# Down projection of an attention + SwiGLU kernel: sums on VectorE in a fixed order, another product order, the first tile's value multiplied out of PSUM

## The chip, the cores and the metric

The kernel runs on one core of a Trainium2 chip (trn2). The metric is the device time of one execution in microseconds (us). The profile is of one execution; its engines are PE (TensorE matmul), PEld (TensorE weight load), DVE (VectorE), ACT (ScalarE), POOL (GpSimd) and SP (SyncE, which only issues transfers here).

## What is computed

An attention with rotary embedding over q, k, v of shape (4, 8, 576, 64), whose output is read as a matrix x of 2304 tokens by 512, and a gated projection on it:

```python
q_rot, k_rot = (rotate(q), rotate(k))
scores = scale * np.matmul(q_rot, k_rot.transpose(0, 1, 3, 2))
...
attn = np.exp(scores)
attn = attn / (np.sum(attn, axis=-1, keepdims=True) + 1e-09)
return np.matmul(attn, v).astype(np.float32)
...
g = x @ w_gate
silu = g * (1.0 / (1.0 + np.exp(-g)))
val = x @ w_val
return (silu * val @ w_out).astype(np.float32)
```

`w_gate` and `w_val` are 512 x 1536, `w_out` is 1536 x 512. All of it is fp32.

## The kernel before

Every fp32 factor is split into a high part (a cast by ACT) and a low part (source minus high part, a subtraction, most of them on DVE), and every product is three matmuls: high by high, high by low, low by high. Matmuls are 128x128 by 128x384: a block of tokens has BK = 384 columns.

Three stretches of the program matter here.

**Plain stage** (about 282 to 341 us). The attention is over and x stands in SBUF. For the first of NFP = 6 pairs of features, twelve units of plain matmuls (`mm`, L789) compute gate and value of one 128x384 block each. `ev` (L793 to L807) empties a unit's two PSUM banks: ACT applies Silu to the gate (L804), ACT copies the value (L805), and one transfer of 384 KB takes both to `hv` in DRAM. The value is multiplied on later. DVE at the same time makes splits and sums for the next stage. All engines run in program order there.

**Up stage** (about 337 to 563.7 us). The other five feature pairs go through a Strassen-Winograd scheme with seven products per 2x2 block (`unit`, L809; `finish`, L865). Tokens come in three pairs of blocks, taken in the order 1, 2, 0. PE and SP run in the order written; ACT, DVE and POOL are ordered by the tile scheduler. `Down.lead` gives a list of items (token pair, product, function) that are hooked into the last unit: the first loads and splits of the next stage. This is called the passage below.

**Down stage** (`Down.run`, L1399 to L1459). Three tiles of tokens, again seven products each, so 21 steps. A product has two halves j (128 output features each) of 6 x 3 matmuls, 36 in all, at L1437; 756 in the stage. Names that come up:

- `load` (L1358, L1360) and `late` (L1363): the four blocks B11, B12, B21, B22 of a tile, each 128 x 6 x 384, come from DRAM (`hv` for the gate of the first feature pair, `hd` for the others, `sg` from SBUF where the last pair of the first tile is still there). `vload` (L1351) brings the value of the first feature pair, `mult` (L1367) multiplies it on: on DVE for the first tile, on POOL for the others.
- `form` (L1377, L1378): for the step after the current one, the sum of blocks if that product needs one (L1373, one instruction of 128x2304, on DVE in the first tile and for one product of each tile, otherwise on POOL), then the split of the source in two halves of 128x1152: cast on ACT (L1377), subtraction on DVE (L1378). The results stand in two sets of buffers, so the split of a step can begin when the product before the running one is done.
- `osplit` (L1344 on ACT, L1345): the split of the seven `w_out` operands, 128x1536, in the first tile; the subtraction for all but the first two is on POOL.
- after a product: PSUM is copied by ACT (L1442, L1444, L1447) or added to an SBUF tile by DVE (L1440); POOL adds one more pair for `o22`. Results go out over SP (L1397).

ACT, DVE and POOL are ordered by the scheduler here too: it places each instruction by a model of times. In the lists of buffers, `dB`, `dT` are raw blocks and sums, `dH`, `dW`, `dWF` the split ones, `dO` split `w_out` operands, `du`, `dz`, `do` the tiles after a product.

Of the kernel before, what the change touches and what calls it, by code (L numbers as in the profile page):

```python
# [925 lines left out]
def attn_swiglu(ctx: ExitStack, tc: tile.TileContext, qk, vr, wg, wv, wo, main, tail, out):  # L926
# [4 lines left out]
    hd = [dr.tile([NFP - 1, 128, 4, BK], FP32, name=f"hd{p}") for p in range(3)]  # L931
    hv = [dr.tile([128, 4, 2, BK], FP32, name=f"hv{p}") for p in range(3)]
# [4 lines left out]
    moe = Moe(tc, keep, pl, yd, rd, hd, hv, od, wg, wv, wo, out)  # L937
# [168 lines left out]
    strassen(moe, J, S, Z).run()  # L1106
# [195 lines left out]
MULT = {4: ("B11",), 6: ("B21", "B12")}  # L1302
RAW = {"B11": ("T1h", 0), "B21": ("T1l", 2), "B12": ("T2h", 1), "B22": ("T2l", 3)}


class Down:
    def __init__(self, moe):
        self.moe, self.nc = moe, moe.nc
        self.raw, self.O, self.H, self.t, self.V = {}, {}, {}, {}, {}

    def lead(self):
        ve = self.nc.vector
        return [
            (0, 0, self.first), (0, 1, lambda: self.oload(0, slice(0, 5))), (0, 5, lambda: self.osplit(0, ve, slice(0, 5))),
            (1, 0, lambda: self.vload(0, "xb1")), (1, 0, lambda: self.load(0, "B11")),
            (1, 0, lambda: self.load(0, "B21")), (1, 4, lambda: self.late("B11")), (1, 4, lambda: self.late("B21")),
            (1, 4, lambda: self.oload(0, slice(5, 6))), (1, 4, lambda: self.oload(1)),
            (2, 0, lambda: self.load(0, "B12")), (2, 0, lambda: self.load(0, "B22")), (2, 0, lambda: self.late("B12")),
            (2, 0, lambda: self.late("B22")), (2, 0, lambda: self.mult(0, "B11", ve)),
            (2, 1, lambda: self.osplit(0, ve, slice(5, 6))),  # L1320
            (2, 1, lambda: self.form(0, ve)), (2, 4, lambda: self.mult(0, "B21", ve)), (2, 5, lambda: self.osplit(1, ve)),
        ]

    def first(self):
# [3 lines left out]
        self.O[0] = [x[:, 2304:3840].rearrange("p (f d) -> p f d", f=NFP) for x in (w, f)]  # L1328

    def oload(self, k, z=slice(0, NFP)):  # L1330
        a = self.moe.again
        if k == 4:
            self.O[4] = [self.w1[:, 2304:3840].rearrange("p (f d) -> p f d", f=NFP), a("FO", [128, NFP, 256], F32R, "dO")]
        elif k == 5:
            self.O[5] = [self.moe.r_p.tile([128, NFP, 256], F32R, name="R"), a("xm1", [128, NFP, 256], F32R, "dO")]
        elif k:
            s = {1: ("xa1h", "xa1l"), 2: ("xa2h", "xa2l"), 3: ("T0l0", "T0l1"), 6: ("xm2", "xm0")}[k]
            self.O[k] = [a(x, [128, NFP, 256], F32R, "dO") for x in s]
# [3 lines left out]
    def osplit(self, k, e, z=slice(0, NFP)):  # L1342
        Oh, Ol = (x[:, z] for x in self.O[k])
        self.nc.scalar.copy(Oh, r32(Ol))  # L1344
        e.tensor_tensor(out=Ol, in0=r32(Ol), in1=r32(Oh), op=ALU.subtract)  # L1345

    def vload(self, n, slot=None):
        m, p = self.moe, ORDER[n]
        for x in range(2):
            v = m.raw_p.tile([128, 2, BK], FP32, name="raw") if slot is None else                 m.again(f"{slot}{'hl'[x]}", [128, 2, BK], FP32, "dV")  # L1350
            self.nc.sync.dma_start(out=v, in_=m.hv[p][:, 2 * x:2 * x + 2, 1])  # L1351
            self.V[x] = v
# [16 lines left out]
    def form(self, s, e, se=None):
        k = s % 7  # L1370
        if k in SUMS:
            o, a, b = SUMS[k]
            se.tensor_tensor(out=self.raw[o], in0=self.raw[a], in1=self.raw[b], op=ALU.subtract)  # L1373
        src = self.raw[FORM[k]]
        hi, lo = self.H[s % 2]
        for z in (slice(0, 3), slice(3, NFP)):
            self.nc.scalar.copy(hi[:, z], src[:, z])  # L1377
            e.tensor_tensor(out=lo[:, z], in0=src[:, z], in1=r32(hi)[:, z], op=ALU.subtract)  # L1378

    def post(self, name, slot):  # L1380
        t = self.t[name] = self.moe.again(slot, [128, 2, BK], FP32, "d" + name)
        return t

    def open(self):
# [102 lines left out]
```

## Time and profile before

| | |
|---|---|
| runs | 724.43, 726.43, 725.01 us; median 725.01 |
| the profiled execution | 725.75 us, of which the profile's span is 724.0 us |
| PE busy over the span | 687.5 us (95%) |
| DVE, ACT, POOL busy | 593.7, 426.0, 541.0 us |
| first matmul of the Down stage | 563.69 us |
| first matmul of its second and third tile | 621.50, 671.99 us |
| start of the last matmul | 720.15 us |

The span is what the profiler saw of the execution; the execution's own time is 1.75 us longer, and it lies 0.74 us above the median. Times inside the program are counted from the start of the span. In a list of instructions the bracket at the end tells how long the engine was idle before it and what ended that; in a list of groups the idle time stands behind the second bar. PEclk is TensorE's granted clock, 1.00 for 2.4 GHz and 0.5 for 1.2 GHz; a value between is a stretch with both.

### The profile page before, as it was taken

The page shows a single profiled execution, that of the slowest core. Times are in us where ns is not written, and L with a number is a line of the kernel's source. Part 1 is how long each engine was busy: PE and PEld are TensorE (multiplying, and loading weights), DVE is VectorE, ACT ScalarE, POOL GpSimd, SP SyncE. Part 2 cuts the span into 40 slices and gives each one's busy share as a digit, 9 for nine tenths or more (in the row PEclk, how much of TensorE's full clock was granted, in tenths as well). Part 3 has the DMA queues.
Part 4 walks back from the last instruction along what each step waited for, and adds up shares of the span by engine and source line. Part 5 has one row for each costly group of instructions (what it writes and reads, how often), then busy time and mean ns, then how long its engine had stood idle before and what let it go on. Part 6 is the DMA issues. An engine that isn't in the chain of part 4 may idle for free. (4 is left out here: it accounts for less than half of the span.)

```text
span 724.0 us, 12703 instructions
## 1 busy us (share of the span) xinstructions
PE 687.5 (95%) x4414; PEld 668.3 (92%) x4414; DVE 593.7 (82%) x848; ACT 426.0 (59%) x873; POOL 541.0 (75%) x498
## 2 busy tenths in 40 slices
PE   7999999999999999997999999999999869899898
PEld 6999999999999998987999999999999768899897
DVE  5889898898888886849888979889886999498593
ACT  5899998888888885456444434444343454343341
POOL 8899799999999865749978695886846458544731
PEclk9999999999999999999999999999999989999999
DMA  6797899779888895962225354463557950733501
GB/s 197 209 223 204 219 226 254 202 212 251 225 204 202 201 265 159 212 215 88 80 95 190 103 178 178 146 205 108 197 189 265 377 185 12 251 115 112 177 12 65
DMA packets 80607, 130.47 MB, mean 180 GB/s; under 512 B 17168, under 2 KB 55968, under 8 KB 80544
## 3 DMA queue, kind: packets, MB, share of 16 engines
q1 hardware_dynamic: 76640, 121.52, 58.6%
q10 hardware_dynamic: 3904, 8.15, 3.0%
q8 instruction: 35, 0.57, 0.3%
q14 instruction: 28, 0.23, 0.1%
HBM read 69.27 MB, written 35.46 MB: 145 GB/s over the span
## 5 line engine op out<-in xcount | busy, mean ns | idle before, releaser
L364 DVE TENSOR_REDUCE nmt<-sc 128x1 f32<-128x576 f32 x144 | 108.2, 751 | 20.2 <-PE sc L349 18.9
L382 ACT ACTIVATE E<-sc,nmt 128x576 f32<-128x576 f32 x128 | 97.6, 762 | 2.3 <-DVE nmt L364 2.3
L1437 PE MATMUL ch<-dW,dO 128*128 128x384 f32 x252 | 78.4, 354 | 3.7 <-ACT du L1442 2.0
L425 PE MATMUL tr<-ident,E 128*128 128x128 f32 x512 | 77.0, 273 | 0.4 <-DVE ET1l L427 0.2
L425 PEld LDWEIGHTS tr<-ident,E 128*128 128x128 f32 x512 | 61.2, 141 | 3.3 <-PE tr L289 1.3
L206 POOL TENSOR_TENSOR t<-X,tab 128x256 f32<-128x256 f32 (+2 forms) x94 | 54.0, 596 | 9.4 <-DMA X<-in_qk_dram 5.7
L349 PE MATMUL sc<-QK 128*128 128x288 f32 x240 | 58.7, 326 | 1.3 <-ACT E L382 0.4
L691 POOL TENSOR_TENSOR W<-WF,W 128x1024 fp32r<-128x1024 f32 x20 | 47.9, 2408 | 11.5 <-ACT W L691 11.5
L426 ACT CAST ET2h<-tr 128x512 fp32r<-128x512 f32 x80 | 47.2, 590 | 15.6 <-PE tr L425 15.4
L427 DVE TENSOR_TENSOR ET2l<-tr,ET2h 128x512 fp32r<-128x512 f32 x80 | 53.3, 683 | 2.2 <-ACT ET2h L426 2.0
L1437 PEld LDWEIGHTS ch<-dW,dO 128*128 128x128 f32 x252 | 49.9, 202 | 5.0 <-ACT du L1442 2.4
L1437 PE MATMUL ch<-dH,dO 128*128 128x384 f32 x180 | 50.6, 339 | 1.4 <-DVE dO L1345 0.9
L349 PE MATMUL sc<-N,QZ 128*128 128x288 f32 x240 | 51.4, 296 | 0.0
L208 POOL TENSOR_TENSOR rot<-rot,t 128x512 f32<-128x512 f32 (+2 forms) x47 | 47.0, 999 | 3.7
L427 DVE TENSOR_TENSOR ET1l<-tr,ET1h 128x512 fp32r<-128x512 f32 x64 | 43.0, 685 | 6.8 <-ACT ET1h L426 6.5
L207 POOL TENSOR_TENSOR rot<-X,tab 128x512 f32<-128x512 f32 (+2 forms) x47 | 47.3, 1006 | 0.0
L837 PE MATMUL ch<-T0h,W 128*128 128x384 f32 x160 | 44.1, 337 | 1.1 <-DVE sg L813 0.5
L426 ACT CAST ET1h<-tr 128x512 fp32r<-128x512 f32 x64 | 36.9, 597 | 13.1 <-PE tr L425 12.9
L837 PE MATMUL ch<-T2h,W 128*128 128x384 f32 x160 | 44.0, 336 | 0.6 <-DVE sg L813 0.6
L837 PE MATMUL ch<-T1h,W 128*128 128x384 f32 x160 | 43.9, 335 | 0.0
L465 PE MATMUL pv<-ET2h,VS 128*128 128x320 f32 x128 | 40.8, 328 | 1.0 <-ACT ET2h L426 0.9
L841 ACT COPY u<-ch 128x384 f32<-128x384 f32 x30 | 14.3, 477 | 45.6 <-PE ch L837 40.8
(338 smaller groups left out, 2396.3 us busy)
## 6 DMA issues: line engine op xcount, KB each, us to landing
QK<-N SPq DMA_DIRECT2D x64, 288.0 KB, 4.3
hd<-sg SPq DMA_DIRECT2D x12, 768.0 KB, 4.1
X<-in_qk_dram SPq DMA_DIRECT2D x15, 576.0 KB, 4.9
yd<-Y SPq DMA_DIRECT2D x31, 256.0 KB, 4.4
dB<-hd SPq DMA_DIRECT2D x8, 960.0 KB, 7.6
raw<-in_moe_w_gate_dram SPq DMA_DIRECT2D x12, 512.0 KB, 5.0
raw<-in_moe_w_val_dram SPq DMA_DIRECT2D x12, 512.0 KB, 3.9
Xab<-yd SPq DMA_DIRECT2D x32, 192.0 KB, 4.4
```

The costliest lines, as they stand in the source:

```text
L206: e.tensor_tensor(out=sel(t2, u), in0=sel(x, w), in1=tb(Sn, u), op=ALU.mult)
L207: e.tensor_tensor(out=o, in0=x, in1=tb(C, slice(0, D)), op=ALU.mult)
L208: e.tensor_tensor(out=o, in0=o, in1=t2, op=ALU.add)
L349: nc.tensor.matmul(ps[:, g, 0:288], l, rr[:, o + g * 288:o + (g + 1) * 288], start=(x == 0), stop=(x == len(terms) - 1))
L364: nc.vector.tensor_reduce(out=nmcol, in_=ps[:, :, 0:288], axis=AX.XY, op=ALU.max, negate=True)
L382: nc.scalar.activation(out=E.rearrange("p (a b) -> p a b", a=2), in_=ps[:, :, 0:288], func=ACTF.Exp, bias=nmcol, scale=1.0, accum_out=self ...
L425: nc.tensor.transpose(ps[:, c], E[:, o + c * 128:o + (c + 1) * 128], self.ident)
L426: nc.scalar.copy(dst[0], src)
L427: nc.vector.tensor_tensor(out=dst[1], in0=src, in1=r32(dst[0]), op=ALU.subtract)
L691: return [lambda: self.nc.scalar.copy(h, f), lambda: le.tensor_tensor(out=l, in0=f, in1=r32(h), op=ALU.subtract)]
L837: nc.tensor.matmul(acc, l[:, w, c * 128:(c + 1) * 128], r, start=(n == 0 and k not in ONTO), stop=(n == 5), skip_group_check=True)
L1437: nc.tensor.matmul(ps, l[:, f, d], r[:, f], start=(a == k and f == 0 and x == 0), stop=(f == NFP - 1 and x == 2), skip_group_check=True)
```

## The change

- Down stage: ACT and DVE also run in the order of the program. All sums of blocks are made by DVE, in halves of 128x1152 (`sums`, L1371); the subtractions of `osplit` are made by DVE in two pieces (L1352); the posts are on ACT (L1437) and DVE (L1439). POOL has no instruction in the stage.
- Another order of products (`FORM`, `OFORM`), with sums that are made from other blocks and in other places, and with PSUM banks that carry sums on from product to product (`BANK`). The intermediate tiles `u` and `z` go.
- Plain stage: `ev` multiplies the value straight from PSUM onto the Silu on DVE (L801), and 192 KB go to `hd`, which now holds all six feature pairs. `hv`, `vload` and `mult` go; a block is one load (L1359), with `late` (L1362) for the first tile.
- Passage: the items of `lead` in another order. Two stores of the last feature pair (`hd[2]`, `hd[0]`) move from the end of the up stage on ACT's queue to SP's (L1403, L1415).

The number and the order of the matmuls ahead of the Down stage are the same, and the stage has 756 as before.

```diff
 def ev(self, u, ps):
...
-        nc.scalar.activation(out=sv[:, 0], in_=ps[0], func=ACTF.Silu)
-        nc.scalar.copy(sv[:, 1], ps[1])
+        sv = self.sv.pop() if u in (2, 3, 8, 9) else self.ld_p.tile([128, 2, BK], FP32, name="Xab")[:, 0]
+        nc.scalar.activation(out=sv, in_=ps[0], func=ACTF.Silu)
+        nc.vector.tensor_tensor(out=sv, in0=ps[1], in1=sv, op=ALU.mult)
         p, b = divmod(3 * s + t, 2)
-        (nc.sync if u else nc.scalar).dma_start(out=self.hv[p][:, 2 * f + b], in_=sv)
+        (nc.sync if u else nc.scalar).dma_start(out=self.hd[p][0][:, 2 * f + b], in_=sv)
...
-        if (fp, p) != (NFP - 1, ORDER[0]):
-            (nc.sync if fp < NFP - 1 else nc.scalar).dma_start(out=self.hd[p][fp - 1], in_=g)
+        if fp < NFP - 1:
+            nc.sync.dma_start(out=self.hd[p][fp], in_=g)
...
-    strassen(moe, J, S, Z).run()
+    dn = strassen(moe, J, S, Z)
+    with tc.manual_schedule(engines={mybir.EngineType.Activation, mybir.EngineType.DVE}):
+        dn.run()
...
-SUMS = {2: ("TT", "B12", "B11"), 3: ("TT", "B22", "TT"), 4: ("B12", "B22", "B12"), 6: ("TT", "B21", "TT")}
-FORM = ("B11", "B21", "TT", "TT", "B12", "B22", "TT")
-OFORM = ((0, 0), (0, 1), (2, 0), (2, 1), (2, 2), (2, 3), (1, 0))
-LOAD = {2: ("B11",), 5: ("B21", "B12"), 6: ("B22",)}
+FORM = ("B11", "B21", "B22", "TT", "B11", "B12", "B21")
+OFORM = ((0, 0), (0, 1), (2, 3), (2, 2), (2, 1), (2, 0), (1, 0))
+BANK = "XZWYXXY"
+SUM = {3: ("TT", "B22", "B12", ALU.subtract), 4: ("B11", "TT", "B11", ALU.add),
+       5: ("B12", "B22", "B11", ALU.subtract), 6: ("B21", "B21", "B11", ALU.subtract)}
+COPY = {0: "o11", 2: "o12", 3: "o22", 4: "o21"}
+ADD = {1: ("o11",), 5: ("o22", "o12"), 6: ("o21",)}
...
+            (0, 0, self.first), (0, 0, lambda: self.oload(0, slice(0, f))), (0, 2, lambda: self.oload(0, slice(f, NFP))),
+            (0, 4, lambda: self.osplit(0)),
+            (1, 0, lambda: self.load(0, "B11")), (1, 0, lambda: self.late("B11")),
+            (1, 0, lambda: self.load(0, "B21")), (1, 2, lambda: self.late("B21")),
+            (1, 2, lambda: self.oload(1)), (1, 2, lambda: self.oload(2)),
+            (1, 4, lambda: run(self.form(0))), (1, 5, lambda: self.osplit(1)),
+            (2, 0, lambda: self.load(0, "B22")), (2, 0, lambda: self.late("B22")),
+            (2, 0, lambda: self.load(0, "B12")), (2, 0, lambda: self.late("B12")), (2, 0, lambda: self.oload(3)),
+            (2, 1, lambda: self.osplit(2)), (2, 5, lambda: self.osplit(3)),
...
     def run(self):
...
-            if s + 1 < N:
-                n1, k1 = divmod(s + 1, 7)
-                if n == 0 and 0 < k < 6:
-                    self.osplit(k + 1, po)
-                self.form(s + 1, ve, ve if n1 == 0 or k1 == 3 else po)
+            for f in zip(self.sums(s + 2), self.form(s + 1)):
+                run(list(f))
+            if n == 0 and 1 < k < 5:
+                self.osplit(k + 2)
+            if s == 2:
+                nc.sync.dma_start(out=m.hd[0][NFP - 1], in_=m.G[0])
...
+                if k in COPY:
+                    ac.copy(t[COPY[k]], ps)
+                for o in ADD.get(k, ()):
+                    ve.tensor_tensor(out=t[o], in0=ps, in1=t[o], op=ALU.add)
+                    self.out(n, o, j)
```

Three places show how instructions move. The first is SP's order in the passage, where the blocks of the first tile are loaded; `od` is `w_out`, `sg` the last feature pair in SBUF. Before:

```order
L1351 DMA dV<-hv_64 128x2x384 x2
L1358 DMA dB_7046<-hv_64 128x384
L1360 DMA dB_7046<-hd_61 128x4x384
L1358 DMA dB_7049<-hv_64 128x384
L1360 DMA dB_7049<-hd_61 128x4x384
L1363 DMA dB_7046<-sg 128x384
L1363 DMA dB_7049<-sg 128x384
L1340 DMA dWF<-od_66 128x256
L1340 DMA dO<-od_66 128x6x256
L1358 DMA dB_7116<-hv_64 128x384
L1360 DMA dB_7116<-hd_61 128x4x384
```

And with the change:

```order
L1359 DMA dB<-hd_61 128x5x384
L1362 DMA dB<-sg 128x384
L1359 DMA dB<-hd_61 128x5x384
L1362 DMA dB<-sg 128x384
L1346 DMA dO<-od_63 128x6x256
L1346 DMA dO<-od_65 128x6x256
L1359 DMA dB<-hd_61 128x5x384
L1362 DMA dB<-sg 128x384
```

The two loads of values are gone, a block is two transfers in place of three, and a second `w_out` operand stands ahead of the third and fourth block. The second place is DVE in a tile after the first, from one product with a sum to the next. Before:

```order
L1378 TENSOR_TENSOR dW_7185<-dT,dH 128x1152 x2
L1373 TENSOR_TENSOR dT<-dB_7510,dT 128x2304
L1378 TENSOR_TENSOR dWF<-dT,dW_6979 128x1152 x2
L1378 TENSOR_TENSOR dW_7185<-dB_7463,dH 128x1152 x2
L1440 TENSOR_TENSOR du<-ch,du 128x384
```

And with the change:

```order
L1371 TENSOR_TENSOR dB<-dB 128x1152
L1381 TENSOR_TENSOR dW_7189<-dB,dH 128x1152
L1371 TENSOR_TENSOR dB<-dB 128x1152
L1381 TENSOR_TENSOR dW_7189<-dB,dH 128x1152
L1439 TENSOR_TENSOR do_7191<-ch,do_7191 128x384 x2
```

Each half of a sum now stands directly ahead of a half of the split for the product one earlier, and two adds from PSUM close a step. The third place is DVE in the plain stage, where the multiplication of `ev` has come in behind a conversion of weights (L754); before, the next row stood directly behind it:

```order
L754 TENSOR_TENSOR WF<-raw,aux 128x512
L801 TENSOR_TENSOR sv<-ch,sv 128x384 x2
L663 TENSOR_TENSOR aux<-aux,T2h 128x384
```

The rows of L801 are the twelve new instructions that DVE carries for ACT's twelve copies.

## Rows read from the trace of the kernel before

**Rows 1.** Page, busy time, share of the span and instructions of each engine.

```profile
PE 687.5 (95%) x4414; PEld 668.3 (92%) x4414; DVE 593.7 (82%) x848; ACT 426.0 (59%) x873; POOL 541.0 (75%) x498
```

**Rows 2.** Windows: us, PE, PEld, DVE, ACT, POOL busy, PEclk, DMA share, GB/s.

```profile
316.00:341.00 25.00, 22.00 (x120) 20.72 (x120) 21.11 (x24) 17.54 (x31) 16.85 (x8) 1.00 0.35 139
...
563.60:621.50 57.90, 48.24 (x254) 45.62 (x253) 52.21 (x30) 25.41 (x26) 32.93 (x12) 0.94 0.56 191
621.50:672.00 50.50, 46.71 (x254) 45.43 (x254) 36.33 (x24) 19.26 (x21) 26.54 (x10) 0.97 0.46 154
672.00:720.50 48.50, 46.28 (x253) 45.31 (x252) 32.20 (x21) 14.77 (x17) 21.80 (x6) 0.96 0.21 75
```

**Rows 3.** Window of L1437 alone: us, PE busy, PEld busy, PEclk, DMA share, GB/s.

```profile
701.51:714.08 12.57, 12.57 (x74) 12.55 (x73) 1.00 0.13 48
```

**Rows 4.** Timeline of PE, Down stage: start us, us, line, tiles.

```profile
563.69 0.35 PE L1437 MATMUL ch<-dW 128*128 128x384 f32 x1
...
621.50 0.33 PE L1437 MATMUL ch<-dH,dW 128*128 128x384 f32 x1
...
671.99 0.34 PE L1437 MATMUL ch<-dW 128*128 128x384 f32 x1
...
720.15 0.34 PE L1437 MATMUL ch<-dW,dO 128*128 128x384 f32 x1
```

**Rows 5.** Waits of PE, 563 to 724 us: total us, times, longest us.

```profile
PE ch L1437 <- DVE dWF L1378: 9.2, 4, 3.3
PE ch L1437 <- DVE dW L1378: 2.6, 3, 1.0
PE ch L1437 <- ACT du L1442: 2.0, 1, 2.0
PE ch L1437 <- DVE dO L1345: 0.9, 1, 0.9
PE ch L1437 <- ACT dH L1377: 0.5, 1, 0.5
```

**Rows 6.** Timeline of DVE, first tile of the Down stage.

```profile
569.57 1.75 DVE L1345 TENSOR_TENSOR dO<-dO 128x1536 fp32r<-128x1536 f32 x1
...
592.92 2.63 DVE L1378 TENSOR_TENSOR dW<-dT,dH 128x1152 fp32r<-128x1152 f32 x2 [1.27 <-ACT dH L1377]
...
596.74 2.55 DVE L1373 TENSOR_TENSOR dT<-dB,dT 128x2304 f32<-128x2304 f32 x1
599.21 4.67 DVE L1378 TENSOR_TENSOR dWF<-dB,dW 128x1152 fp32r<-128x1152 f32 x1
603.80 0.55 DVE L1440 TENSOR_TENSOR du<-ch,du 128x384 f32<-128x384 f32 x1
```

**Rows 7.** Timeline of POOL beside it.

```profile
597.88 4.77 POOL L1345 TENSOR_TENSOR dO<-dO,R 128x1536 fp32r<-128x1536 f32 x1 [8.65 <-ACT R L1344]
602.61 4.62 POOL L1345 TENSOR_TENSOR dO<-dO 128x1536 fp32r<-128x1536 f32 x1
```

**Rows 8.** Largest group of DVE, 563 to 724 us: busy us, mean ns, idle before.

```profile
L1378 DVE TENSOR_TENSOR dW<-dB,dH 128x1152 fp32r<-128x1152 f32 x12 | 25.8, 2155 | 2.7 <-ACT dH L1377 2.5
```

**Rows 9.** Window of the passage, columns as in the second group.

```profile
549.00:571.40 22.40, 20.96 (x120) 20.31 (x119) 17.25 (x22) 9.01 (x12) 10.84 (x7) 1.00 1.04 361
```

**Rows 10.** Timeline of ACT: a cast of w_out, the casts behind it, a copy.

```profile
575.14 1.48 ACT L1344 CAST dO<-dO 128x1536 fp32r<-128x1536 f32 x1 [4.52 <-DMA dO<-od]
576.53 2.20 ACT L1377 CAST dW<-dT 128x1152 fp32r<-128x1152 f32 x2
578.64 0.47 ACT L1444 COPY do<-ch 128x384 f32<-128x384 f32 x1
```

**Rows 11.** Timelines of PE, ACT and DVE where the plain stage ends.

```profile
343.77 0.65 PE L837 MATMUL ch<-xa1h,W 128*128 128x384 f32 x1 [2.99 <-ACT u L841]
...
341.49 1.47 ACT L691 CAST T0h<-R 128x1536 fp32r<-128x1536 f32 x1 [2.92 <-POOL R L697]
...
344.71 0.54 DVE L813 TENSOR_TENSOR u<-ch,u 128x384 f32<-128x384 f32 x1
```

More of the change, by code (lines that the diff above doesn't have):

```diff
@@ L930, in attn_swiglu @@
     rd = dr.tile([B, 36, 128], FP32, name="rd")
-    hd = [dr.tile([NFP - 1, 128, 4, BK], FP32, name=f"hd{p}") for p in range(3)]
-    hv = [dr.tile([128, 4, 2, BK], FP32, name=f"hv{p}") for p in range(3)]
+    hd = [dr.tile([NFP, 128, 4, BK], FP32, name=f"hd{p}") for p in range(3)]
     od = [dr.tile([NFP, 128, n, 256], FP32, name=f"od{n}") for n in (2, 1, 4)]
@@ L936, in attn_swiglu @@
     keep, pl, mctx = ExitStack(), ExitStack(), ExitStack()
-    moe = Moe(tc, keep, pl, yd, rd, hd, hv, od, wg, wv, wo, out)
+    moe = Moe(tc, keep, pl, yd, rd, hd, od, wg, wv, wo, out)
     actx = ExitStack()
@@ L1308, in __init__ @@
         self.moe, self.nc = moe, moe.nc
-        self.raw, self.O, self.H, self.t, self.V = {}, {}, {}, {}, {}
+        self.raw, self.O, self.H, self.t = {}, {}, {}, {}
+        self.where = {"B11": "T1h", "B21": "T1l", "B22": "T2h", "B12": "T2l", "TT": "T0h"}
     def lead(self):
-        ve = self.nc.vector
+        f = NFP - 1
         return [
[L1314 to L1321, printed above, removed]
+            (0, 0, self.first), (0, 0, lambda: self.oload(0, slice(0, f))), (0, 2, lambda: self.oload(0, slice(f, NFP))),
[7 more added lines that the diff above has]
+            (2, 1, lambda: self.osplit(2)), (2, 5, lambda: self.osplit(3)),
         ]
@@ L1327, in first @@
         self.H[0] = [x[:, 0:2304].rearrange("p (f q) -> p f q", f=NFP) for x in (w, f)]
-        self.O[0] = [x[:, 2304:3840].rearrange("p (f d) -> p f d", f=NFP) for x in (w, f)]
+        o = [x[:, 2304:3840].rearrange("p (f d) -> p f d", f=NFP) for x in (w, f)]
+        self.O[0] = [[o[0][:, z] for z in THIRD], o[1]]
+        hi = [m.raw_p.tile([128, 4, 256], F32R, name="raw")[:, 0:3] for _ in range(2)]
+        self.O[1] = [hi, m.again("FO", [128, NFP, 256], F32R, "dO")]
     def oload(self, k, z=slice(0, NFP)):
-        a = self.moe.again
@@ L1332, in oload @@
[L1332 to L1338, printed above, removed]
+        if k > 1:
+            a = lambda x: self.moe.again(x, [128, NFP, 256], F32R, "dO")
+            if k == 5:
+                s = self.w1[:, 2304:3840].rearrange("p (f d) -> p f d", f=NFP), a("xm1")
+            elif k == 6:
+                s = self.moe.r_p.tile([128, NFP, 256], F32R, name="R"), a("xm2")
+            else:
+                s = [a(x) for x in {2: ("xa1h", "xa1l"), 3: ("xa2h", "xa2l"), 4: ("T0l0", "T0l1")}[k]]
+            self.O[k] = [[s[0][:, x] for x in THIRD], s[1]]
@@ L1339, in oload, with osplit @@
         h, x = OFORM[k]
         self.nc.sync.dma_start(out=r32(self.O[k][1])[:, z], in_=self.moe.od[h][z, :, x].rearrange("f p d -> p f d"))
[L1342 to L1352, printed above, removed]
+    def osplit(self, k):
+        hi, lo = self.O[k]
+        for h, z in zip(hi, THIRD):
+            self.nc.scalar.copy(h, r32(lo)[:, z])
+            self.nc.vector.tensor_tensor(out=lo[:, z], in0=r32(lo)[:, z], in1=r32(h), op=ALU.subtract)
@@ L1369, in form @@
[L1369 to L1376, printed above, removed]
+        k = BLK[b]
+        r = self.raw[n, b] = m.again(self.where[b], [128, NFP, BK], FP32, "dB")
+        f = NFP - 1 if n == 0 else NFP
+        self.nc.sync.dma_start(out=r[:, 0:f], in_=m.hd[p][0:f, :, k].rearrange("f p q -> p f q"))
@@ new lines, in late, with sums @@
+    def late(self, b):
+        self.nc.sync.dma_start(out=self.raw[0, b][:, NFP - 1], in_=self.moe.G[ORDER[0]][:, BLK[b]])
+    def sums(self, s):
+        n, k = divmod(s, 7)
+        if s >= 21 or k not in SUM:
+            return [lambda: None] * 2
+        if k == 3:
+            self.raw[n, "TT"] = self.moe.again(self.where["TT"], [128, NFP, BK], FP32, "dB")
+        o, a, b = (self.raw[n, x] for x in SUM[k][:3])
+        return [lambda z=z: self.nc.vector.tensor_tensor(out=o[:, z], in0=a[:, z], in1=b[:, z], op=SUM[k][3]) for z in THIRD]
@@ L1377, in form, with go @@
+    def form(self, s):
+        n, k = divmod(s, 7)
+        if s >= 21:
+            return [lambda: None] * 2
+        src, (hi, lo) = self.raw[n, FORM[k]], self.H[s % 2]
+        def go(z):
             self.nc.scalar.copy(hi[:, z], src[:, z])
[L1378 to L1382, printed above, removed]
+            self.nc.vector.tensor_tensor(out=lo[:, z], in0=src[:, z], in1=r32(hi)[:, z], op=ALU.subtract)
+        return [lambda z=z: go(z) for z in THIRD]
```

91 lines of the change are left out of this document (26 added, 65 removed).

## The prediction

> **What bounds the kernel now.** I begin with the page's busy times: PE works for 687.5 of the 724.0 us, DVE for 82%, POOL for 75% [rows 1]. So PE is the bound on the whole, and what can be won is what PE loses. Next come the windows by stage: look at the PE column against the length. Down to the first matmul of the Down stage little is missing; its three tiles last 57.9, 50.5 and 48.5 us, for the same 252 matmuls each, and PEclk reads 0.94, 0.97 and 0.96 there [rows 2].
>
> What would a tile take undisturbed? The window from 701.51 to 714.08 holds two whole products, 72 matmuls by the program (the row also counts those cut by its edges), without an idle gap and at the 2.4 GHz level: 12.57 us, so 174.6 ns for one matmul, 6.285 us for a product, 44.0 us for seven [rows 3]. By the starts of the tiles and the last matmul with its 0.34 us, the tiles take 621.50 - 563.69 = 57.8, 671.99 - 621.50 = 50.5 and 720.49 - 671.99 = 48.5 us [rows 4]. They lose **13.8, 6.5 and 4.5 us, 24.8 in all**. That is the whole of what this part of the change can win at the pace shown.
>
> Who holds PE up? The waits of PE in the stage sum to 15.2 us, of which 9.2 + 2.6 are for subtractions of the split on DVE [rows 5]. The rest goes with the clock: the PEclk shares come to 0.06 x 57.9 + 0.03 x 50.5 + 0.04 x 48.5 = 6.9 us, part of each tile at 1.2 GHz; 2.7 us I can't assign.
>
> Why is DVE late? Two subtractions of 1152 with nothing on POOL take 2.63 us, 1.31 each; the same instruction takes 4.67 us when it begins at 599.21 [rows 6], while POOL's subtraction runs from 597.88 to 602.65, and it ends 1.23 us, about one duration, after POOL's end [rows 7]. An add from PSUM keeps its 0.55 us while POOL works [rows 6, 7]. So a long DVE instruction stands still for as long as POOL's does, if both its inputs are in SBUF. The Trainium skill states this as a rule (SBUF — State Buffer, "Who interferes with whom": such an instruction and a GpSimd one that reads SBUF share one pair of ports, which is locked for a whole instruction); the trace agrees.
>
> **The Down stage after the change, step by step.** POOL has nothing to do there, so I take the price without POOL for each instruction: 1.31 us for a subtraction of 1152 and, as half of the sum's 2.55 us, 1.28 us for half a sum [rows 6].
>
> A step with a sum has on DVE two halves of a sum, two of a split and at most two adds, which I book with 0.55 us: 2 x 1.28 + 2 x 1.31 + 0.55 = **5.7 us against 6.285 us** of PE. (The step with two adds per half, 2.2 us, has no sum beside them.) The split of a step may begin when the product before the running one is done; its second half is needed only 9 matmuls, 1.6 us, into its product, which covers the hand-over between engines. ACT has two casts, 2.20 us a pair, and at most two copies of 0.47 us [rows 10], 3.1 us. So tiles 2 and 3 keep PE fed. Their loads are issued at the fourth to sixth product for a use two or more products, 12.6 us, later; at the 361 GB/s of the passage the 1152 KB of a block are 3.3 us [rows 9]. Nothing else is late: they win **6.5 and 4.5 us**, the time at 1.2 GHz included, which stood beside waits.
>
> The first tile also carries three `osplit`, 1.75 us each on DVE [rows 6]: in their steps DVE needs about 5.7 - 0.55 + 1.75 = 6.9 us, and these steps have no adds but one, so it loses 0.6 to 0.7 us in each of three, some 2 us, less what it had in hand. I book **1.5 us**; the ends are 0 and 4 (no slack, and PE's clock falls). With it the tile wins 13.8 - 1.5 = **12.3 us**.
>
> What of the passage? Today ACT stands 4.52 us for a `w_out` operand (landed at 575.1), and the casts of the third product's sum stand behind it, until 576.53 [rows 10], when by 563.69 + 2 x 6.285 = 576.3 that product is due. With the change the first product with a sum is the fourth, due at 582.5: 6.3 us more room. DMA is the limit ahead of it: the queues moved 361 GB/s from 549 to 571.4 with a DMA share of 1.04, full [rows 9]. With the change four blocks (4 x 960 KB and 4 x 192 KB) and two `w_out` operands (768 KB) come before the first sum, 6.3 MB: 17.4 us at that rate. I let them start 1.6 us into that window, behind the last piece of the first operand: 568. DVE comes to its first sum today at 571.3, behind a split of `w_out` [rows 6]; two multiplications ahead of it go and part of another split comes, so about 570.5 (an estimate). That leaves 2.3 us; beyond it each us of delay costs one. The two stores of 768 KB that go from ACT's queue to SP's stand behind these loads, and two loads of later `w_out` operands behind the stores, needed from the fifth product (588.8) on; I book nothing.
>
> **The plain stage.** ACT loses twelve copies of 0.47 us [rows 10], DVE gains twelve multiplications from PSUM, 0.55 us each like the add [rows 6]. The price lies between two ends. At its end PE waits 2.99 us for ACT's copy of `u`, which stood behind a cast that waited 2.92 us for POOL's `R` [rows 11], and the first matmuls after it take 0.65 us for 0.34: 1.2 GHz. If ACT's shorter queue removes that, it is -4.5 us. DVE is in a row from 327 to 349 there (21.11 of 25 us in its window [rows 2]); four multiplications come in before the add of `u` at 344.71 [rows 11], 2.2 us, and if it passes whole to PE with as much again at the lower clock, it is +5. POOL's operations there are held by DVE's and not by ACT, so `R` comes when it came: I take 0.
>
> Less goes out by 192 KB per unit, hidden. The tail after the last product is one add, 0.55 us, and one store in both.
>
> **Sum.** 725.75 - 12.3 - 6.5 - 4.5 = 702.4 us for an execution like the profiled one. That one is 0.74 us above the median, so **701.7 us**. With the plain stage from -4.5 to +5 and tile 1 from +1.5 to -2.5, not all at once, the forecast's own range is 697.5 to 706.
>
> **The rivals.**
> - **The first tile keeps half its loss** (13%). For it: the passage's 2.3 us of slack stand on a start at 550.6 that hangs on buffers coming free, and DVE has no spare in that tile. Two transfers 5 us late, or two waits of 3.3 us each with a slow spell, cost 7 to 10 us: 708 to 712, say 711. Against it: the first sum is a product later.
> - **DVE becomes the bound: slower** (3%). If the long price came from something other than POOL, a transfer or ACT's and PE's accesses, an instruction of 1152 would keep the mean of its largest group, 2.16 us [rows 8], say 2.2. A step with a sum would take 4 x 2.2 + 0.55 = 9.35 us, 3.07 above PE, in 12 steps: +36.8 us in place of -23.3, so about 738 from 701.7. It decides from 12 x (4d + 0.55 - 6.285) = 23.3 on, d = 1.92 us. Against it: the 2.63 us pair and its like, at the same transfers.
> - **The waits only move** (4%). Sums and splits in one fixed order put the split behind a sum that waits for a block; if each tile goes on losing 6 to 7 us there, with the tile-1 loss half kept, it ends between 712 and 724, within 0.3% at the upper end. Against it: each load has two products' time.
> - **The plain stage pays 4 us or more** (3%): 706 to 708, by the upper bound above.
> - **A faster pace** (3%). The 174.6 ns are of one stretch, and its row doesn't say what limits it; if that goes with POOL's work, matmuls come closer. To leave the range at 697.5 that takes 4.2 us over 756 matmuls, 169.0 ns or less. Against it: PE and PEld are busy for all 12.57 us of the row [rows 3]. The Trainium skill (TensorE: Matmul & The Clock Gate, "Back-to-back issue gap") gives an isolated gap of N / 2.4 + 2.5 ns, for 384 columns 162.5 ns; by it 756 matmuls would take 9.1 us less, estimated 693. The trace disagrees as far as it goes, with 174.6 ns.
>
> **How the numbers follow.** The forecast has 74%. The range that leaves out less than two in ten goes from 697.5 to 711: the forecast's own, the plain stage's price and most of the first rival. What a measurement of this kernel tells from no change is 0.3%, 2.2 us. Only the slow DVE lies above that (3%); half of the moved waits within it (2%); faster 95%.
>
> **What would show it.** Right: seven products of 6.3 us from start to start in tiles 2 and 3; waits of PE in the stage under 3 us, and PEclk at 1.00; the instructions of 1152 on DVE at 1.3 us on average; POOL idle after about 568; twelve multiplications of 0.55 us in the plain stage, with the wait of 2.99 us near its end still there or less. Wrong: splits on DVE over 1.9 us with POOL idle; a PE wait for DVE in each of the steps two to five of every tile; the first matmul of the Down stage later than 566, which would put the loss before the stage; tile 1 over 50 us, with DVE or ACT waiting for a transfer.

## The result, and the profile after

The changed kernel takes **699.88 us** (median of four runs, 699.19 to 701.12) against 725.7 us (four runs of the kernel before): a ratio of 0.9648, 95% interval 0.9626 to 0.9669. The forecast was 701.7 us, its range 697.5 to 711. Later, on another occasion, it was 699.64 us, ratio 0.9639 (0.9615 to 0.9663).

The profiled execution took 701.12 us with a span of 699.3 us, 24.6 us less than the profiled one before. First its windows, with the columns of [rows 2]; the three in the middle are the tiles of the Down stage:

```profile
316.00:341.00 25.00, 21.62 (x117) 19.73 (x116) 24.05 (x32) 16.00 (x26) 19.01 (x9) 1.00 0.17 60
341.00:367.00 26.00, 23.31 (x127) 21.91 (x128) 22.66 (x37) 13.13 (x20) 21.91 (x19) 1.00 0.27 79
...
561.90:607.70 45.80, 44.84 (x253) 43.88 (x253) 43.95 (x43) 26.66 (x33) 3.59 (x2) 1.00 0.82 278
607.70:651.80 44.10, 44.10 (x254) 44.10 (x253) 32.27 (x30) 19.27 (x22) 0.00 (x0) 1.00 0.43 144
651.80:696.40 44.60, 44.23 (x254) 43.91 (x252) 30.15 (x29) 15.79 (x19) 0.00 (x0) 1.00 0.10 36
```

PE is busy for all 44.10 us of the second tile, PEclk reads 1.00 in each, POOL's column is empty from the second tile on. The starts of the tiles and the last matmul on PE's timeline, as in [rows 4]:

```profile
561.90 0.35 PE L1433 MATMUL ch<-dW 128*128 128x384 f32 x1
...
607.73 0.34 PE L1433 MATMUL ch<-dH,dW 128*128 128x384 f32 x1
...
651.85 0.34 PE L1433 MATMUL ch<-dW 128*128 128x384 f32 x1
...
695.70 0.33 PE L1433 MATMUL ch<-dW,dO 128*128 128x384 f32 x1
```

So the tiles take 45.8, 44.1 and 44.2 us, 134.1 in all, where it was 57.8, 50.5 and 48.5, 156.8 in all [rows 4]. What PE waited for in the stage, and the groups of DVE there, against [rows 5] and [rows 8]:

```profile
PE ch L1433 <- DVE dW L1381: 0.8, 2, 0.5
PE ch L1433 <- DVE dWF L1381: 0.2, 1, 0.2
```

```profile
L1371 DVE TENSOR_TENSOR dB<-dB 128x1152 f32<-128x1152 f32 x24 | 32.3, 1347 | 0.0
L1381 DVE TENSOR_TENSOR dW<-dB,dH 128x1152 fp32r<-128x1152 f32 x20 | 28.3, 1431 | 8.1 <-ACT dH L1380 8.1
L1381 DVE TENSOR_TENSOR dWF<-dB,dW 128x1152 fp32r<-128x1152 f32 x20 | 26.7, 1349 | 7.8 <-ACT dW L1380 7.8
L1439 DVE TENSOR_TENSOR do<-ch,do 128x384 f32<-128x384 f32 x24 | 12.6, 549 | 12.2 <-PE ch L1433 12.2
```

15.2 us of waits have become 1.0, and DVE's subtraction of 1152 takes 1.35 us where its mean was 2.16 (1.43 in the group that holds the slow first pair, of which more under the first tile). The account between the two profiled executions: 22.7 us in the Down stage; 1.8 us ahead of it, since the first matmul of the stage starts at 561.9 in place of 563.7; 0.2 us behind the last matmul. Together 24.7, less 0.1 us outside the span.

### The profile page after: what moved, and what is told of

It reads as the page before. It is cut to its first block, busy times and chain, and to the rows that moved or that the text cites. A ratio compares the mean times of both kernels' runs of the same rounds, so it can differ in the third digit from the quotient of the medians.

```text
span 699.3 us, 12687 instructions
## 1 busy us (share of the span) xinstructions
PE 679.3 (97%) x4414; PEld 662.6 (95%) x4414; DVE 580.2 (83%) x885; ACT 425.3 (61%) x873; POOL 464.8 (66%) x473
## 4 chain that ended last, share of the span: by engine, by line
PE 62%; POOL 12%; DMA 9%; DVE 8%; issue 4%; ACT 3%; SPq 0%; ACTq 0%; DVEq 0%; POOLq 0%
PE ch L833 26%; PE ch L1433 14%; PE sc L349 7%; PE pv L465 7%; PE tr L425 5%; POOL R L697 2%; DVE dB L1371 2%; POOL t L206 1%; POOL rot L208 1%; DMA Xab<-yd 1%; DMA dO<-od 1%; POOL rot L207 1%; DMA raw<-in_moe_w_gate_dram 1%; PE tr L289 1%; POOL Z L697 1%
## 5 line engine op out<-in xcount | busy, mean ns | idle before, releaser
L1433 PE MATMUL ch<-dW,dO 128*128 128x384 f32 x216 | 63.8, 336 | 0.5 <-DVE dW L1381 0.5
L833 PE MATMUL ch<-T2h,W 128*128 128x384 f32 x160 | 44.2, 337 | 1.5 <-DVE sg L809 1.5
L1433 PE MATMUL ch<-dH,dO 128*128 128x384 f32 x156 | 45.4, 337 | 0.0
L837 ACT COPY u<-ch 128x384 f32<-128x384 f32 x30 | 14.3, 478 | 47.7 <-PE ch L833 47.5
L349 PEld LDWEIGHTS sc<-QK 128*128 128x128 f32 x240 | 36.9, 190 | 4.0 <-ACT E L382 3.9
```

What stands on the lines that cost most here:

```text
L349: nc.tensor.matmul(ps[:, g, 0:288], l, rr[:, o + g * 288:o + (g + 1) * 288], start=(x == 0), stop=(x == len(terms) - 1))
L833: nc.tensor.matmul(acc, l[:, w, c * 128:(c + 1) * 128], r, start=(n == 0 and k not in ONTO), stop=(n == 5), skip_group_check=True)
L1433: nc.tensor.matmul(ps, l, r[:, f], start=(new and f == 0 and x == 0), stop=(f == NFP - 1 and x == 2), skip_group_check=True)
```

## The experiments

Eleven edits were run, and the changed kernel once more. Since PE's stretch ahead of the Down stage varies by some us between executions, the table gives, from each trace, the start of the stage and the lengths of the tiles (from first matmul to first matmul, the last to the end of the last matmul) beside the time.

| kernel | median us | ratio to before (95%) | stage starts | tile 1 | tile 2 | tile 3 |
|---|---|---|---|---|---|---|
| before | 725.7 | | 563.7 | 57.8 | 50.5 | 48.5 |
| before, sums on DVE | 717.64 | 0.9889 (0.9871 to 0.9907) | 563.8 | 57.4 | 46.1 | 44.2 |
| before, POOL empty | 710.91 | 0.9794 (0.9773 to 0.9816) | 562.9 | 53.2 | 44.2 | 44.2 |
| changed, first profile | 699.88 | 0.9648 (0.9626 to 0.9669) | 561.9 | 45.8 | 44.1 | 44.2 |
| changed, again | 699.64 | 0.9639 (0.9615 to 0.9663) | 559.9 | 45.8 | 44.1 | 44.2 |
| sums on POOL in tiles 2, 3 | 704.68 | 0.9722 (0.9683 to 0.9761) | 558.8 | 45.8 | 45.6 | 48.4 |
| idle work on POOL | 705.51 | 0.9732 (0.9695 to 0.9769) | 559.3 | 45.8 | 46.6 | 47.5 |
| scheduler orders ACT, DVE | 710.03 | 0.9783 (0.9742 to 0.9823) | 562.1 | 54.9 | 44.1 | 44.2 |
| sum in the step of its split | 720.62 | 0.9941 (0.992 to 0.9961) | 560.6 | 55.2 | 50.2 | 49.5 |
| value copied, then multiplied | 706.05 | 0.9729 (0.9704 to 0.9753) | 568.1 | 45.8 | 44.1 | 44.2 |
| block B12 loaded later | 700.76 | 0.9651 (0.9624 to 0.9678) | 560.3 | 46.7 | 44.1 | 44.2 |
| w_out splits a step later | 700.3 | 0.965 (0.9627 to 0.9672) | 561.2 | 46.3 | 44.1 | 44.2 |
| w_out splits on POOL | 707.82 | 0.975 (0.9729 to 0.9771) | 562.4 | 51.8 | 44.1 | 44.2 |
| last multiplication moved | 697.31 | 0.9618 (0.9597 to 0.9639) | 557.8 | 44.6 | 44.3 | 44.2 |

**What an empty POOL is worth alone.** Two edits of the kernel before; the second has both lines, the first only the upper:

```diff
-                self.form(s + 1, ve, ve if n1 == 0 or k1 == 3 else po)
+                self.form(s + 1, ve, ve)
...
-        ve, po, ac = nc.vector, nc.gpsimd, nc.scalar
+        ve, po, ac = nc.vector, nc.vector, nc.scalar
```

> The kernel before with one thing of the change: all sums of the Down stage on DVE, in one piece of 2304; the scheduler places them. POOL keeps its multiplications, the splits of w_out in tile 1 and the adds for o22. If POOL's sums are what cost tiles 2 and 3 their 11.0 us: these two come to 44 to 46 us each, 714 to 719 us. If the lead of the sums and the new order of products matter as much, the long waits stay (a sum of 2.6 us ahead of its split): 720 to 726 us.

> The kernel before with nothing on POOL in the Down stage: sums, splits of w_out, multiplications and the add for o22 on DVE, everything else as before. If an idle POOL is the main thing: the stage at 136 to 141 us in place of 156.8, 705 to 710 us. If the order of products with its sums a step ahead is needed for it: 145 to 155 us, 714 to 724 us; tile 1 decides, since DVE has there 7 x 2.7 + 4 x 2.6 + 5 x 1.8 + 5.5 us and the casts of w_out hold up those of the sums on ACT.

The sums alone bring tiles 2 and 3 from 99.0 to 90.3 us together, and the time lies in the range of the first theory; with the rest of POOL's work on DVE they stand at 88.3, as in the changed kernel. There the stage takes 141.6 us and the median is 710.91, both just above what the first theory gave: an idle POOL is the larger part, but not all. Nothing else of the change is needed for these two tiles. The first tile is another matter: 53.2 us, 4.6 of the 12.0 us that the change wins there. Its waits with POOL empty:

```profile
PE ch L1437 <- DVE dW L1378: 2.4, 1, 2.4
PE ch L1437 <- ACT dH L1377: 2.1, 1, 2.1
PE ch L1437 <- DVE dWF L1378: 1.7, 1, 1.7
PE ch L1437 <- DVE dO L1345: 0.9, 1, 0.9
```

**POOL's work back in the changed kernel**, in three ways. Sums on POOL in tiles 2 and 3:

```diff
-        return [lambda z=z: self.nc.vector.tensor_tensor(out=o[:, z], in0=a[:, z], in1=b[:, z], op=SUM[k][3]) for z in THIRD]
+        e = self.nc.gpsimd if n else self.nc.vector
+        return [lambda z=z: e.tensor_tensor(out=o[:, z], in0=a[:, z], in1=b[:, z], op=SUM[k][3]) for z in THIRD]
```

> The changed kernel, but in tiles 2 and 3 the halves of the sums are made by POOL, still a step ahead of their split; ACT and DVE keep their fixed order. Theory (POOL's instructions hold up the long ones on DVE): POOL has four steps of two halves per tile, 2.6 us each by half of 5.13 us for a whole sum; splits on DVE that meet one take 3 to 4 us in place of 1.35, tiles 2 and 3 lose 3 to 6 us each again, about 706 to 712 us. Rival (the fixed order with sums a step ahead is what removed the waits): POOL's 5.2 us per step fit into 6.3, the tiles stay at 44.1 us, 699 to 701 us.

Tiles 2 and 3 lose 1.5 and 4.2 us: the sign is the theory's, but tile 2 and the median (704.68) lie below its ranges. DVE has 16 long instructions fewer, and still the tiles are slower, as each split takes longer, in groups of the whole stage:

```profile
L1382 DVE TENSOR_TENSOR dW<-dB,dH 128x1152 fp32r<-128x1152 f32 x20 | 43.6, 2210 | 10.1 <-ACT dH L1381 10.1
L1382 DVE TENSOR_TENSOR dWF<-dB,dW 128x1152 fp32r<-128x1152 f32 x20 | 42.6, 2160 | 3.6 <-ACT dW L1381 3.6
```

Here a late sum could be the cause as well. So the second: work on POOL on which nothing depends.

```diff
+                if n and j == 0:
+                    r = t[("o11", "o11", "o12", "o22", "o21", "o22", "o21")[k]]
+                    for x in range(4):
+                        nc.gpsimd.tensor_tensor(out=self.scr[:, x % 2], in0=r, in1=r, op=ALU.add)
```

> The changed kernel, with work on POOL that nobody needs: in tiles 2 and 3, behind the first half of each product, four additions of 128x384 from an output tile into a scratch tile, about 28 us per tile, as much as POOL had there before. The output is the reference's. Theory (POOL's instructions hold up the long ones on DVE): of DVE's 29 us of long instructions per tile most meet POOL's, 29 + 28 = 57 us against 44; 8 to 13 us lost per tile, 716 to 726 us, the mean of a subtraction of 1152 at 1.9 us or more. Rival (nothing hangs on POOL being idle; the waits went with the data that came from POOL): 699 to 702 us and 1.35 us.

The sign is the theory's, the size is not: 2.5 and 3.4 us per tile in place of 8 to 13. The groups of DVE and POOL in the stage tell why:

```profile
L1371 DVE TENSOR_TENSOR dB<-dB 128x1152 f32<-128x1152 f32 x24 | 40.2, 1676 | 0.0
L1381 DVE TENSOR_TENSOR dW<-dB,dH 128x1152 fp32r<-128x1152 f32 x20 | 34.3, 1731 | 3.6 <-ACT dH L1380 3.6
L1381 DVE TENSOR_TENSOR dWF<-dB,dW 128x1152 fp32r<-128x1152 f32 x20 | 32.7, 1651 | 1.8 <-ACT dW L1380 1.8
```

```profile
L1445 POOL TENSOR_TENSOR scr<-do 128x384 f32<-128x384 f32 x56 | 82.6, 1509 | 52.8 <-ACT do L1438 44.4 <-DVE do L1440 8.5
```

DVE's three groups grew by 107.2 - 87.3 = 19.9 us, of which its idle time in the two tiles took up the most: by the windows of the changed kernel 11.8 and 14.4 us were free. Where both engines work without a gap, they take turns, as one row of each shows; the last row is an addition that meets no long DVE instruction:

```profile
636.82 1.98 DVE L1371 TENSOR_TENSOR dB<-dB 128x1152 f32<-128x1152 f32 x1
...
635.65 1.94 POOL L1445 TENSOR_TENSOR scr<-do 128x384 f32<-128x384 f32 x1
...
611.07 0.82 POOL L1445 TENSOR_TENSOR scr<-do 128x384 f32<-128x384 f32 x1
```

A meeting there costs DVE 1.98 - 1.35 = 0.63 us and POOL 1.94 - 0.82 = 1.12 us. So POOL was held up more than DVE; I had booked all of it on DVE, and at the whole length of POOL's instruction.

The third puts the splits of the last three `w_out` operands in tile 1 on POOL:

```diff
+        e = self.nc.gpsimd if k > 3 else self.nc.vector
...
-            self.nc.vector.tensor_tensor(out=lo[:, z], in0=r32(lo)[:, z], in1=r32(h), op=ALU.subtract)
+            e.tensor_tensor(out=lo[:, z], in0=r32(lo)[:, z], in1=r32(h), op=ALU.subtract)
```

> The changed kernel, but the subtractions of the last three w_out operands in tile 1 are on POOL again, where nothing else runs. If tile 1 loses its 1.8 us because DVE has 7.1 us of work per step, the 1.8 us per step leave DVE and tile 1 comes to 44.2 to 44.6 us, 1.2 us faster, 698.5 us. If POOL's instructions hold up the long ones on DVE, each of the six gives back about as much or more: tile 1 at 46 to 49 us, 700 to 703 us.

Tile 1 takes 51.8 us, 5.9 more, though DVE has 5.4 us less to do: the second theory's sign, and more than its 46 to 49 us. That the `w_out` operands themselves came late from POOL is not the reason, since all that PE waited for in the stage is DVE's splits of blocks:

```profile
PE ch L1434 <- DVE dW L1382: 3.3, 3, 2.3
PE ch L1434 <- DVE dWF L1382: 1.8, 1, 1.8
```

The timelines of DVE and POOL in the fourth and fifth product:

```profile
587.59 3.00 DVE L1382 TENSOR_TENSOR dWF<-dB,dW 128x1152 fp32r<-128x1152 f32 x1
590.51 3.01 DVE L1372 TENSOR_TENSOR dB<-dB 128x1152 f32<-128x1152 f32 x1
593.44 1.34 DVE L1382 TENSOR_TENSOR dWF<-dB,dW 128x1152 fp32r<-128x1152 f32 x1
```

```profile
587.19 5.11 POOL L1353 TENSOR_TENSOR dO<-dO,dW 128x768 fp32r<-128x768 f32 x2 [4.54 <-ACT dW L1352]
```

Each of the two DVE instructions that meet POOL's pair takes 1.66 us longer than the next, which meets nothing. DVE gave up 0.94 us for a piece and pays 1.66.

**The fixed order.** Without the manual schedule of the Down stage:

```diff
-    with tc.manual_schedule(engines={mybir.EngineType.Activation, mybir.EngineType.DVE}):
-        dn.run()
+    dn.run()
```

> The changed kernel, but ACT and DVE in the Down stage are ordered by the scheduler again; the same instructions. Theory (POOL being empty is the main part): 699 to 704 us, since every instruction of 1152 keeps 1.35 us. Rival (the fixed order is the main part): waits of 3 us and more come back in each tile, 708 to 715 us.

Both were half right: tiles 2 and 3 do not change, tile 1 takes 54.9 us, 9.0 more, and the time falls into the rival's range. The means of DVE's groups are as in the changed kernel; the order is other. In the fourth product, from 581.4, PE waits 4.5 and 2.3 us for the two halves of a split; on DVE's timeline each half (L1380) stands behind both halves of a sum for a later product (L1370) and behind splits of `w_out` (L1351):

```profile
579.29 1.81 DVE L1351 TENSOR_TENSOR dO<-dO 128x768 fp32r<-128x768 f32 x2
581.02 2.61 DVE L1370 TENSOR_TENSOR dB<-dB 128x1152 f32<-128x1152 f32 x2
...
584.90 1.34 DVE L1380 TENSOR_TENSOR dW<-dB,dH 128x1152 fp32r<-128x1152 f32 x1
...
587.03 2.61 DVE L1370 TENSOR_TENSOR dB<-dB 128x1152 f32<-128x1152 f32 x2
589.57 0.94 DVE L1351 TENSOR_TENSOR dO<-dO,dW 128x768 fp32r<-128x768 f32 x1
590.44 1.34 DVE L1380 TENSOR_TENSOR dW<-dB,dH 128x1152 fp32r<-128x1152 f32 x1
```

So in the tile where DVE has no time to spare, the order decides; in the others the scheduler's order does as well as the fixed one.

**The lead of the sums.**

```diff
-            for f in zip(self.sums(s + 2), self.form(s + 1)):
+            for f in zip(self.sums(s + 1), self.form(s + 1)):
```

> The changed kernel, but the halves of a sum stand directly ahead of the split of the same product, not a step earlier. The work of DVE is the same. If DVE's busy time decides: no change, 699 to 701 us. If the chain decides (half a sum 1.35, cast 1.16 with 0.2 of hand-over, subtraction 1.35, twice one after the other, 8.2 us and an add against 6.3 us of PE): about 2 us lost in each of 12 steps, 720 to 726 us.

All but 1.9 of the stage's 22.7 us are gone again, with POOL empty and the same work on DVE. The chain decides, but not with 2 us in each of twelve steps: in each tile one product (14.9, 10.0 and 9.9 us in place of 6.3) takes the larger part. There PE's timeline shows a wait I had not reckoned, of a kind that makes 9.1 of the stage's 15.7 us of waits:

```profile
601.55 0.69 PE L1433 MATMUL ch<-dH,dW 128*128 128x384 f32 x1 [5.18 <-ACT do L1437]
```

ACT's copies of PSUM stand in order behind casts that now wait for sums, and a product that goes on in the same bank waits for the copy. So the 20.7 us are the price of a late sum under the fixed order and with banks carried on; what it costs without these two was not run.

**The first tile.** Three edits. The splits of the last `w_out` operands a step later:

```diff
-            if n == 0 and 1 < k < 5:
-                self.osplit(k + 2)
+            if n == 0 and 2 < k < 6:
+                self.osplit(k + 1)
```

> The changed kernel, but the splits of the last three w_out operands stand one step later, one step ahead of their use, so that the last falls into a step without a sum. Theory (tile 1's loss of 1.8 us is DVE's 7.1 us per step in three steps, in two now): tile 1 at 45.0 to 45.4 us in place of 45.8, 699 to 699.7 us. Rival (the loss hangs on hand-overs or transfers): no change of tile 1 within 0.2 us; if a split is now late for its product, 46 to 48 us.

The theory missed, and the last case named holds: tile 1 takes 46.3 us, 0.5 more. PE now waits 1.0 us in all for two of the `w_out` splits (a row "DVE dO L1352" among its waits), and DVE's work in a row is no shorter. Block B12 later:

```diff
-            (2, 0, lambda: self.load(0, "B12")), (2, 0, lambda: self.late("B12")), (2, 0, lambda: self.oload(3)),
+            (2, 0, lambda: self.oload(3)),
...
         self.oload(4)
+        self.load(0, "B12")
+        self.late("B12")
         self.oload(5)
```

> The changed kernel, but the load of block B12 of the first tile stands behind two more w_out operands (2 x 768 KB, 4.3 us at 361 GB/s). The first sum needs it, at 570.2 us in the changed kernel with the block there at 568.9. Theory: it lands near 573 to 575 or later since the operands wait for buffers, DVE stands 3 to 6 us at the first sum, and with the split behind it; PE waits 2 to 5 us in the third product, 702 to 706 us. Rival (the passage has more slack than reckoned): under 1 us, 700 to 701.

The first sum waits for it, but little:

```profile
566.88 3.55 DVE L1352 TENSOR_TENSOR dO<-dO 128x768 fp32r<-128x768 f32 x4
571.29 1.36 DVE L1371 TENSOR_TENSOR dB<-dB 128x1152 f32<-128x1152 f32 x1 [0.85 <-DMA dB<-hd]
```

DVE had put another split of `w_out` ahead of that sum (four pieces, not two), and its stage began 1.6 us earlier. The third product takes 8.2 us in place of 6.25, with 1.4 us of waits for its split, less than the theory's 2 to 5; the fourth and fifth, which that other split no longer delays, win 1.0 back. Tile 1 loses 0.9 us; the rival's figure was right. Last, an edit that takes away what held DVE up at the start of the stage: the last multiplication of the up stage, on POOL from 564.4, is needed for the third tile only. The lines that build the last `w_out` operand elsewhere in SBUF are left out here.

```diff
+        if (fp, p) == (NFP - 1, ORDER[2]):
+            self.last = g, v
+            return
         nc.gpsimd.tensor_tensor(out=g[:, 1:3], in0=v[:, 1:3], in1=g[:, 1:3], op=ALU.mult)
...
-            if s == 2:
+            if s == 6:
+                g, v = m.last
+                ve.tensor_tensor(out=g[:, 1:3], in0=v[:, 1:3], in1=g[:, 1:3], op=ALU.mult)
+            if s == 7:
                 nc.sync.dma_start(out=m.hd[0][NFP - 1], in_=m.G[0])
```

> The changed kernel, but the last multiplication of the up stage (L865 for the last token pair, 128x768, on POOL at 564.4 us, needed by the third tile only) is made by DVE in the seventh step of the Down stage, where DVE waits for PE; its store stands two steps later than now, and the sixth w_out split is built elsewhere in SBUF. In the changed kernel the two subtractions of 1152 beside it took 4.27 us, without POOL they take 2.68. If tile 1's 1.8 us are DVE's work in a row from 563 us on, the 1.6 us return: tile 1 at 44.2 to 44.8 us in place of 45.8, and the whole about 1.3 us faster, ratio to the kernel before 0.962 to 0.963. If tile 1 hangs on something else (casts on ACT, transfers), tile 1 stays within 0.3 us and the ratio at 0.964 to 0.965.

Tile 1 takes 44.6 us, 1.3 less. The pair of subtractions, in the changed kernel and here:

```profile
564.27 4.27 DVE L1381 TENSOR_TENSOR dW<-dB,dH 128x1152 fp32r<-128x1152 f32 x2
```

```profile
560.18 2.61 DVE L1386 TENSOR_TENSOR dW<-dB,dH 128x1152 fp32r<-128x1152 f32 x2
```

The fourth and fifth product, which lost 0.8 and 0.5 us, lose nothing now; the sixth still loses 0.6. The time is 697.31 us, the lowest measured; its interval still touches that of the changed kernel, so the tile's length in the traces carries the verdict. That the stage began earlier here than in any other trace, at 557.8, I can't assign to the edit: already the first matmul of the up stage, long before the edit acts, stands at 332.2 us here, against 332.4 to 334.4 in the others with this plain stage.

**The plain stage.** What the changed kernel multiplies out of PSUM there is the value of the first feature pair, for all three tiles and not, as the title has it, for the first alone. Here the value is copied by ACT as before and then multiplied from SBUF:

```diff
-        nc.vector.tensor_tensor(out=sv, in0=ps[1], in1=sv, op=ALU.mult)
+        nc.scalar.copy(val, ps[1])
+        nc.vector.tensor_tensor(out=sv, in0=val, in1=sv, op=ALU.mult)
```

> The changed kernel, but in the plain stage ACT copies the value out of PSUM as before, and DVE multiplies from SBUF; so ACT has its twelve copies again and a PSUM bank does not wait for DVE. If the 1.8 us by which the Down stage began earlier come from ACT's shorter queue, it begins 1 to 2 us later, 701 to 702 us. If they are chance of that stage (clock spell, or a wait that moves), 699 to 701 us, no difference that five rounds tell.

It costs far more than expected: the stage begins at 568.1, 7.4 us behind the mean of the nine traces that share the changed kernel's plain stage (560.7, from 558.8 to 562.4). The Down stage is unchanged. ACT's copies by themselves are not the cause, since the kernel before has them too and its stage began at 563.4 on the mean of three traces. What changed is DVE. The multiplication out of PSUM in the changed kernel, and POOL's instruction beside it:

```profile
328.32 1.02 POOL L697 TENSOR_TENSOR R<-xm 128x384 f32<-128x384 f32 x1
...
328.50 0.54 DVE L801 TENSOR_TENSOR sv<-ch,sv 128x384 f32<-128x384 f32 x1
```

And the one out of SBUF, with the same POOL instruction beside it:

```profile
329.97 1.02 POOL L697 TENSOR_TENSOR R<-xm 128x384 f32<-128x384 f32 x1
...
330.05 1.37 DVE L803 TENSOR_TENSOR sv<-sv 128x384 f32<-128x384 f32 x1
```

0.54 against 1.37 us for the same elements, three times (1.37, 1.37, 1.34) in a stretch where DVE is never idle. At its end ACT's cast, and the copy of `u` behind it, wait for POOL in the changed kernel and for DVE here, and PE for that copy:

```profile
339.34 1.47 ACT L691 CAST T0h<-R 128x1536 fp32r<-128x1536 f32 x1 [3.29 <-POOL R L697]
...
341.25 0.45 PE L833 MATMUL ch<-xa1h,W 128*128 128x384 f32 x1 [0.96 <-ACT u L837]
```

```profile
343.58 1.47 ACT L691 CAST T0h<-R 128x1536 fp32r<-128x1536 f32 x1 [3.03 <-DVE T2l L691]
...
345.49 0.44 PE L835 MATMUL ch<-xa1h,W 128*128 128x384 f32 x1 [4.76 <-ACT u L839]
```

How much of the 7.4 us the operand in SBUF costs alone is open: the copies came back with it.

## Why the prediction was right, point by point

- **The loss and its size.** The 24.8 us that the tiles lost against 44.0 us each were the right measure: the stage won 22.7, booked were 23.3. Tiles 2 and 3 came to 44.1 and 44.2. The pace held, 44.1 us for 252 matmuls or 175 ns for one, and the rival of a faster one fell. (By the formula of the Trainium skill, TensorE: Matmul & The Clock Gate, "Back-to-back issue gap", a tile would have been 41.0 us, an estimate; 44.1 were measured.)
- **Why DVE was late.** POOL's instructions hold up DVE's long ones: shown by the work for nobody and most plainly by the 3.00 and 1.34 us of the splits on POOL; the two edits of the kernel before show what that is worth in tiles 2 and 3. That DVE stands still for as long as POOL's instruction lasts was too much for the short additions, 0.63 us for 0.82. The prices of 1.31 and 1.28 us held: one instruction lasts 1.35, and in a row one starts every 1.27 us, so a step is 4 x 1.27 + 0.55 = 5.6 us, and even by 1.35 it is under 6.285. DVE as the bound of all steps, the slower rival, fell with it.
- **The first tile.** 1.5 us were booked, 1.8 lost, in the three products named. That these are DVE's work in a row holds. But the prediction put it all on the three splits; 1.3 of the 1.8 us go with POOL's last multiplication, which fell on the first split of the stage and made 4.27 us of 2.61. So the size was right in part by luck. Two more splits of `w_out` stand in DVE's queue in that tile, at 568.5 and 575.7 us; of these the prediction counted only part of the first.
- **The passage.** The first sum began at 570.2 (570.5 predicted), its last block landed at 568.9 (568). The claim that each us beyond 2.3 costs one was too strict: DVE does a split in the meantime.
- **The other rivals.** The first tile did not keep half its loss, and the waits did not move: 1.0 us is left of them in the stage.
- **What was not priced.** The fixed order and the lead of the sums were taken as the way in which the instructions run, not as terms. They are conditions of the gain: 9.0 us of tile 1 hang on the first, 20.7 us of the stage on the second while the order is fixed. The two overlap and don't add up.
- **The plain stage** is the term that was mis-sized: 0 booked, -1.8 us between the two profiled executions, and -2.7 between the means of starts (three traces with the old plain stage, 563.4; nine with the new one, 560.7, from 558.8 to 562.4). The mechanism lay inside the bounds: PE's wait for `u` fell from 2.99 to 0.96 us, though ACT's cast still waited 3.3 us for POOL's `R`, as foreseen, and PEclk in the window behind it rose to 1.00 from 0.93 before:

```profile
341.00:367.00 26.00, 22.05 (x113) 21.09 (x114) 23.11 (x38) 13.29 (x19) 22.32 (x18) 0.93 0.23 70
```

The -1.8 us are a net figure. The first matmul of the up stage starts 2.0 us earlier (334.41 against 336.43), the 61st 3.8 us (347.9 against 351.7), near the -4.5 of the forecast's lower end; 2.0 us are lost again in the up stage, where PE now waits 1.55 us for DVE at 354 us, for 0.59 before:

```profile
354.26 0.44 PE L833 MATMUL ch<-T2h,W 128*128 128x384 f32 x1 [1.55 <-DVE sg L809]
```

- **The sum.** The 1.8 us, 0.2 behind the last matmul and the stage's missing 0.6 take 702.4 to the 701.1 of the profiled execution. The median of the four runs lay another 1.2 us lower, where the forecast had taken 0.7 off; 1.3 and 0.5 us make up the 1.8 us from 701.7 to 699.9. The 0.7 had no ground as it turned out: with a fourth run the kernel before has a median of 725.7, that of its profiled execution. From median to median the change is worth 25.8 us, where 23.3 were booked.

## What to carry to other kernels

When the engine that feeds TensorE is late, look for what stretches its instructions before counting them: here the same subtraction took 1.35 us or 3.0 by what POOL did beside it, and moving all of POOL's work of a stage onto the fuller engine made the stage faster. A PSUM operand keeps a DVE instruction out of that. Where the order on an engine is fixed, make what is needed a step before it is needed: with the same instructions, that was worth 20.7 of 22.7 us here. It is not the only way: in the kernel before with POOL empty, the scheduler's own order kept tiles 2 and 3 at 44.2 us.

## What the runs showed of the hardware that was not expected

- The hold-up works both ways. POOL's additions of 128x384 took 1.94 us between DVE's long instructions, against 0.82 where they met none, and 56 of them cost DVE 19.9 us. The Trainium skill (SBUF — State Buffer, "Who interferes with whom") says that the order of issue decides which of the two is blocked; two engines that take turns, as here, agree with it.
- A 128x384 multiplication on DVE with an operand in PSUM took 0.54 us while POOL worked; with both in SBUF 1.37, 0.56 being its price with POOL idle (555 ns, the mean of eight in the kernel before with POOL empty).
